# Thresholded attention and a two-layer network: where the weights are turned in the first rounds, and how the kernel starts and ends

## The chip, the cores and the metric

The kernel runs on one core of one Trainium2 chip. The core has five engines that each work through their own list of instructions in order: TensorE (PE in the profile; its weight loads are listed apart as PEld), VectorE (DVE), ScalarE (ACT), GpSimd (POOL) and SyncE (SP). They wait for each other only through semaphores. Matrix products land in PSUM, which has eight banks; DMA transfers are issued from a queue of an engine (here SP, ACT and POOL) and run beside the engines. The metric is the device time of one execution, in microseconds (us); lower is better.

## The reference

Eight batches of eight heads, 576 tokens each, 64 numbers to a head. Attention keeps only the scores that lie within `tau` of the row's maximum; its output goes through a network with a leaky ReLU between two layers.

```python
def _attn_ref(q, k, v, tau):                  # (8, 8, 576, 64) each, tau 0.02
    scores = np.matmul(q, k.transpose(0, 1, 3, 2)) / np.sqrt(64)
    thresh = np.max(scores, axis=-1, keepdims=True) - tau
    scores = np.where(scores >= thresh, scores, -1000000000.0)
    scores = scores - np.max(scores, axis=-1, keepdims=True)
    attn = np.exp(scores)
    attn = attn / (np.sum(attn, axis=-1, keepdims=True) + 1e-09)
    return np.matmul(attn, v).astype(np.float32)

def _moe_ref(x, w_in, w_out):                 # (4608, 512), (512, 2048), (2048, 512)
    h = x @ w_in
    g = np.maximum(0.01 * h, h)
    return (g @ w_out).astype(np.float32)
```

Between the two, the heads of a token are laid side by side, so that x has 4608 rows of 512.

## The kernel before

**Steps and rounds.** Heads are taken in pairs (four pairs a batch). The first 512 tokens of a batch are its main part, the last 64 its tail. A step is 128 queries of one pair against all 576 keys; `c` says which half of a block of 256 queries it is, so two steps with c = 0 and c = 1 share one set of weights, a `Pair` object. A batch has 18 steps (16 main, 2 tail), the whole 144. One loop, `while n < N + 7 ...` at the end of the kernel, with counter n, writes the program: a pass through it is called a round here. The order in which a round calls its functions is the order of each engine's list; nothing is moved later (`manual_schedule`).

**Inputs.** q and k come as 32-bit numbers and are used as a sum of two 16-bit halves, high and low (`split_now` with ACT and DVE for the first three pieces; `split_scale`, `split_high`, `split_low` on POOL for others). `turn` then transposes a piece on PE, 8 or 16 small transposes into a PSUM tile `tp` (tag "h", two banks, or "o", one), and copies it to `qT` or `kT` (lines 195, 189, 193), by ACT or by the engine that is given as `copy`. `units` gives the order of pieces: pair 0's k and q, the tail's k, pair 1's k and q, and so on; `first` is that list for batch 0, so that `first[7]` is the fourth pair's k. `load_pair` (line 477) issues a pair's load for batch 0; the first two go out on SP's queue (k) and on ACT's (q).

**A step.** In round n `scores` (L252) makes the step's scores in two PSUM tiles of two banks each, which are all that there are of that kind; so the next scores need DVE's `copy_min` (L260) to have emptied them. That copy also finds the row's extreme. `threshold` (L269 on DVE, L272 on POOL from step 28 on) adds tau. In round n + 1 `exps` makes the exponentials on ACT, for one head directly (L295) and for the other behind a sharp Prelu that drops what is under the threshold (L291, L292); `weights` (L304, DVE) does the dropping for the first head. Both leave their sums in `pr.sum`.

**Dividing and turning.** `recip` (L310, DVE) takes the reciprocals of the sums; `widen` (L313, DVE or POOL) writes them 64 times each into block 9 of the pair's weights `pr.w`, which blocks 0 to 8 fill with the weights of both heads (two times 576). Turned together with the weights, the reciprocals stand where the output needs them. From step 8 on the turning is one DMA transpose for a pair (`turn_w`, L321). The first eight steps are `early`: their weights are turned by PE (`turn_w_pe`, L331) into PSUM tiles `wp` of five blocks ("half" 0 is blocks 0 to 4 in bank "o", half 1 is blocks 5 to 9 in a bank "h") and copied to `wT` (L333). For an early step, `recip` and `widen` come in round n + 1 right behind `weights`, for one c at a time, and `turn_w_pe` in round n + 2. For later pairs they come in the round after, between `copy_min` and `threshold`, through the list `ended`. `pv` (L348) multiplies by v, `evacuate` (L370, L360) scales by block 9 into x; for early pairs this is in round 4, 6, 8 and 10.

**The network and the rest of a round.** `layer1` (L391, L393) and `layer2` (L407, L413) take finished groups of 256 or 128 tokens in small portions, one and two a round, from round 11 on; after the last step only these are left. `store` (L422, L425) sends a finished group out; the very last group is the tail rows of the last two batches, two stores of 64 rows. `idle` (L515) puts filler products on PE, in rounds 0 to 4 and in the even ones to 10 right behind the scores, in rounds 5, 7 and 9 behind the turning; `pool_at`, `turns_at`, `loads_at` and `rows_at` say in which round pieces of the preparation are put.

Of the kernel before, what the change touches and what calls it, by code (L numbers as in the profile page):

```python
# [37 lines left out]
def kernel(  # L38
# [236 lines left out]
    def exps(st):  # L275

        c = st.c
        if c == 0:
            pairs["now"] = pr = Pair()
            pr.w = sb.tile([128, 2, 10, 128], FP16, tag="w", bufs=3, name="w")  # L280
            pr.sum = sb.tile([128, 2, 2], FP32, tag="sum", bufs=3, name="sum")
            pr.n = 2
        st.pair = pr = pairs["now"]
        flat = pr.w[:, c, :, :].rearrange("q n d -> q (n d)")
        st.w = [flat[:, ds(576 * h, 576)] for h in range(2)]
        st.sum = [pr.sum[:, c, h : h + 1] for h in range(2)]
        st.e = sb.tile([128, 576], FP16, tag="e", bufs=2, name="e")
        for h in range(2):
            if h:
                z = st.s[:, h, :]  # L290
                nc.scalar.activation(out=z, in_=z, func=AF.Prelu, bias=st.th[:, h, 0:1], scale=-1.0, alpha=1e20)  # L291
                nc.scalar.activation(out=st.w[h], in_=z, func=AF.Exp, bias=minus_tau[:, :], scale=1.0,  # L292
                                     accum_out=st.sum[h])
            else:
                nc.scalar.activation(out=st.e[:, :], in_=st.s[:, h, :], func=AF.Exp, bias=st.mn[:, h, 0:1],  # L295
                                     scale=-1.0)
# [26 lines left out]

    def turn_w_pe(pr, c):
        if c == 0:
            new_wt(pr)
        for half, copy in enumerate((nc.scalar.copy, nc.scalar.copy if c else nc.vector.tensor_copy)):
            wp = ps.tile([128, 8, 128], FP16, tag="oh"[half], bufs=1 + half, name="wp")
# [69 lines left out]
    def layer2(n):  # L398
# [10 lines left out]
        if r == 7:  # L409
            nm = g.tokens // 128  # L410
            if m == 0:
                g.osb = sb.tile([128, nm, 512], FP32, tag=f"osb{nm}", bufs=2 if nm == 2 else 1, name="osb")
            nc.scalar.activation(out=g.osb[:, m, :], in_=g.o[:, :], func=AF.Copy, bias=0.0, scale=1.0)  # L413
            if m == nm - 1:
                stores.append(g)

    def store():
        g = stores.pop(0)
# [4 lines left out]
        else:  # L423
            for u in range(2):
                nc.sync.dma_start(out=out[ds((b + u) * S + MAIN, 64), :], in_=g.osb[ds(64 * u, 64), 0, :])  # L425

# [4 lines left out]
    def at(d, n, f):  # L431
        d.setdefault(n, []).append(f)
# [46 lines left out]

    load_pair(0, "k", nc.sync)  # L480
    load_pair(0, "q", nc.scalar)
    load_tails(0, "k", (nc.sync, nc.scalar))
# [36 lines left out]
    idle(34)  # L519
    for key in first[:3]:  # L520
        split_now(key)
    turn(first[0])
    turn(first[1], nc.vector.tensor_copy)
    turn(first[2], bank="o")
    idle(5)
# [10 lines left out]
    for n_, key in zip((1, 2, 3, 10), first[5:8] + first[9:]):  # L536
        at(turns_at, n_, lambda key=key: turn(key, nc.vector.tensor_copy if key[2] == "q" else None))

# [5 lines left out]
    while n < N + 7 or l1q or l2q or stores:  # L544
# [24 lines left out]
        if 0 < n < N:  # L569
            threshold(steps[n])  # L570
        if ended:
            widen(ended[0], 0, 2)
            turn_w(ended.pop())
# [4 lines left out]
        if 1 <= n <= N:  # L578
            last = steps[n - 1]
            weights(last)  # L580
            if last.early:
                recip(last.pair, last.c, 1)
                widen(last.pair, last.c, 1, nc.vector if n < 7 else nc.gpsimd)
            elif last.c == 1 and n < 2 * PERB:

# [7 lines left out]
        while stores:  # L593
            store()
        if l1q and l1q[0][3] <= n:
# [47 lines left out]
```

## Time and profile before

Three runs took 492.56, 492.96 and 493.05 us; the median is 492.96.

| | us |
|---|---|
| profiled execution | 492.28 |
| its span, first to last instruction | 490.3 |
| PE busy in the span | 475.4 |
| ACT busy | 432.7 |
| DVE busy | 406.9 |
| POOL busy | 315.2 |

Busy time by stretch of the span (us):

| stretch | PE | DVE | ACT | POOL |
|---|---|---|---|---|
| 0 to 8.7 (loads, first pieces) | 7.17 | 2.88 | 5.19 | 3.30 |
| 8.7 to 24.6 (rounds 0 to 4) | 14.44 | 15.00 | 13.77 | 15.15 |
| 24.6 to 44.2 (rounds 5 to 10) | 16.48 | 18.73 | 19.41 | 16.24 |
| 44.2 to 60 | 13.95 | 15.58 | 15.50 | 11.26 |
| 60 to 80 | 19.61 | 18.67 | 18.70 | 19.19 |
| 130 to 455 | 324.93 | 288.56 | 302.05 | 210.72 |
| 478.6 to 490.3 (last products, stores) | 7.18 | 0.00 | 1.85 | 0.00 |

How to read it: a row of the profile names the engine, the line of the kernel, the instruction, output<-input and the count; in brackets stands the idle time ahead of it and what ended that. Busy shares are means over stages with different limits, so each stage is read by itself. In the chain of waits every piece is what the next one waited for. PE's filler products count as busy, and matmuls are pipelined, so that a busy PE is not one at its peak. In the first rounds PE's busy time holds the filler.

### The profile page before, as it was taken

The page shows a single profiled execution, that of the slowest core. Times are in us where ns is not written, and L with a number is a line of the kernel's source. Part 1 is how long each engine was busy: PE and PEld are TensorE (multiplying, and loading weights), DVE is VectorE, ACT ScalarE, POOL GpSimd, SP SyncE. Part 2 cuts the span into 40 slices and gives each one's busy share as a digit, 9 for nine tenths or more (in the row PEclk, how much of TensorE's full clock was granted, in tenths as well). Part 3 has the DMA queues.
Part 4 walks back from the last instruction along what each step waited for, and adds up shares of the span by engine and source line. Part 5 has one row for each costly group of instructions (what it writes and reads, how often), then busy time and mean ns, then how long its engine had stood idle before and what let it go on. Part 6 is the DMA issues. An engine that isn't in the chain of part 4 may idle for free.

```text
span 490.3 us, 19692 instructions
## 1 busy us (share of the span) xinstructions
PE 475.4 (97%) x8039; PEld 343.6 (70%) x8039; DVE 406.9 (83%) x1217; ACT 432.7 (88%) x784; POOL 315.2 (64%) x534
## 2 busy tenths in 40 slices
PE   8989899999999999999999999999999999999996
PEld 6656666766777777777777777777777777667884
DVE  5999998989989899989899898989899898888100
ACT  6899999899999999999999999999999999999431
POOL 5987799678866686768766686768766673222000
PEclk9999999999999999999999999999999999999999
DMA  8999898989999998999997998999999978768412
GB/s 253 263 206 158 164 204 134 246 168 198 214 190 181 194 233 171 192 190 213 150 221 171 208 199 193 192 172 228 157 211 163 208 128 168 136 116 152 108 45 66
DMA packets 220443, 87.79 MB, mean 179 GB/s; under 512 B 190656, under 2 KB 217280, under 8 KB 220352
## 3 DMA queue, kind: packets, MB, share of 16 engines
q1 hardware_dynamic: 217120, 82.00, 81.8%
q0 software_dynamic: 2688, 4.19, 4.9%
q8 instruction: 63, 1.03, 0.9%
q10 hardware_dynamic: 544, 0.33, 0.2%
q14 instruction: 28, 0.23, 0.2%
HBM read 36.70 MB, written 9.44 MB: 94 GB/s over the span
## 4 chain that ended last, share of the span: by engine, by line
PE 78%; DVE 9%; ACT 4%; POOL 4%; DMA 2%; issue 2%; SPq 0%; POOLq 0%; DVEq 0%; ACTq 0%
PE hp L391 25%; PE o L407 20%; PE sc L252 20%; PE pv L348 7%; DVE s L260 5%; PE osc L407 4%; PE tpr L207 3%; DVE w L304 2%; POOL half L151 1%; DMA wT<-w 1%; DMA raw<-in_q_dram 1%; ACT w L292 1%; ACT e L295 1%; ACT s L291 1%; DVE x L370 1%
## 5 line engine op out<-in xcount | busy, mean ns | idle before, releaser
L260 DVE TENSOR_SCALAR_CACHE_REDUCE s<-sc 128x576 f32<-128x576 f32 x288 | 206.4, 753 | 33.4 <-PE sc L252 31.4
L252 PE MATMUL sc<-kT,qT 64*128 64x288 f16 (+1 forms) x1920 | 135.9, 285 | 4.2 <-DVE s L260 3.1
L391 PE MATMUL hp<-x,win 128*64 128x256 f16 x2048 | 136.7, 275 | 0.5 <-DVE x L370 0.5
L391 PEld LDWEIGHTS <-win 128*64 128x64 f16 x2560 | 118.5, 109 | 23.5 <-issue 17.4
L407 PE MATMUL o<-wout,g 128*64 128x512 f16 x992 | 127.8, 379 | 0.0
L304 DVE SCALAR_TENSOR_TENSOR w<-s,th,e 128x576 f16<-128x576 f32 x144 | 120.3, 835 | 0.5 <-ACT e L295 0.5
L272 POOL TENSOR_SCALAR th<-mn 128x2 f32<-128x2 f32 x116 | 52.7, 454 | 103.0 <-DVE s L260 81.2
L252 PEld LDWEIGHTS <-qT 64*128 64x128 f16 (+1 forms) x1920 | 77.0, 96 | 58.8 <-issue 43.6
L292 ACT ACTIVATE w<-s,minus_tau 128x576 f16<-128x576 f32 x144 | 111.7, 775 | 5.2
L291 ACT ACTIVATE s<-s,th 128x576 f32<-128x576 f32 x144 | 110.3, 766 | 1.9 <-POOL th L272 1.5
L295 ACT ACTIVATE e<-s,mn 128x576 f16<-128x576 f32 x144 | 110.2, 765 | 0.8 <-DVE s L260 0.8
L393 ACT ACTIVATE g<-hp 128x512 f16<-128x512 f32 x144 | 83.9, 583 | 26.2 <-PE hp L391 26.0
L151 POOL TENSOR_TENSOR half<-scaled,half 128x512 f16<-128x512 f32 (+1 forms) x91 | 89.3, 987 | 2.3
L407 PEld LDWEIGHTS <-g 128*64 128x64 f16 x1152 | 65.2, 110 | 29.8 <-issue 0.2
L348 PE MATMUL pv<-wT,v 128*64 128x256 f16 (+1 forms) x960 | 52.0, 247 | 0.5 <-DMA wT<-w 0.5
L348 PEld LDWEIGHTS <-v 128*64 128x64 f16 x960 | 41.6, 111 | 13.8 <-DMA wT<-w 1.2
L143 POOL CAST half<-scaled 128x512 f16<-128x512 f32 (+1 forms) x74 | 44.6, 602 | 4.5
L137 POOL TENSOR_SCALAR scaled<-raw 128x512 f32<-128x512 f32 x62 | 43.6, 702 | 5.4 <-DMA raw<-in_k_dram 4.4
L313 POOL CAST w<-rec 128x256 f16<-128x256 f32 (+1 forms) x70 | 32.0, 457 | 13.3 <-DVE rec L310 7.5
L106 POOL CAST v<-vraw 128x256 f16<-128x256 f32 x64 | 32.2, 532 | 1.3
L370 DVE TENSOR_TENSOR x<-pv,wT 128x256 f16<-128x256 f32 x64 | 27.1, 423 | 4.1 <-PE pv L348 4.0
L292 ACT ACTIVATION_READ_ACCUMULATOR w<-s,minus_tau 128x1 f32 x144 | 26.9, 187 | 0.0
(55 smaller groups left out, 323.1 us busy)
## 6 DMA issues: line engine op xcount, KB each, us to landing
vraw<-in_v_dram SPq DMA_DIRECT2D x16, 512.0 KB, 5.6
out_dram<-osb SPq DMA_DIRECT2D x16, 512.0 KB, 3.4
raw<-in_k_dram SPq DMA_DIRECT2D x14, 512.0 KB, 4.8
raw<-in_q_dram SPq DMA_DIRECT2D x14, 512.0 KB, 4.9
win<-in_moe_w_in_dram POOLq DMA_DIRECT2D x4, 512.0 KB, 7.3
wout<-in_moe_w_out_dram POOLq DMA_DIRECT2D x4, 512.0 KB, 13.8
wT<-w SPq DMA_TRANSPOSE x68, 5.9
raw<-in_k_dram SPq DMA_DIRECT2D x4, 256.0 KB, 5.0
```

The costliest lines, as they stand in the source:

```text
L151: nc.gpsimd.tensor_tensor(out=halves[key][:, 1, i : i + m, :, :], in0=src[:, i : i + m, :, :], in1=halves[key][:, 0, i : i + m, :, :], op= ...
L252: nc.tensor.matmul(out=o, lhsT=lhs, rhs=turned[st.b, "k"][rows, kx, pair, ds(key0, 288)], start=(i == 0), stop=(i == 2), skip_group_check= ...
L260: nc.vector.tensor_scalar(out=st.s[:, h, :].rearrange("p (a b) -> p a b", a=2), in0=st.sc[h][:, :, 0:288], scalar1=-1.0 / UNIT, scalar2=No ...
L272: nc.gpsimd.tensor_scalar(out=st.th[:, :, 0], in0=st.mn[:, :, 0], scalar1=1.0, scalar2=tau_f, op0=AX.mult, op1=AX.add)
L291: nc.scalar.activation(out=z, in_=z, func=AF.Prelu, bias=st.th[:, h, 0:1], scale=-1.0, alpha=1e20)
L292: nc.scalar.activation(out=st.w[h], in_=z, func=AF.Exp, bias=minus_tau[:, :], scale=1.0, accum_out=st.sum[h])
L295: nc.scalar.activation(out=st.e[:, :], in_=st.s[:, h, :], func=AF.Exp, bias=st.mn[:, h, 0:1], scale=-1.0)
L304: nc.vector.scalar_tensor_tensor(out=st.w[0], in0=st.s[:, 0, :], scalar=st.th[:, 0, 0:1], in1=st.e[:, :], op0=AX.is_le, op1=AX.mult, accum ...
L348: nc.tensor.matmul(out=o, lhsT=v16[st.b % 2][:, 2 * c + u if st.tail else st.p, blk, :], rhs=rhs, start=(i == 0), stop=(i == 4), skip_grou ...
L391: nc.tensor.matmul(out=hp[ds(64 * u2, 64), jj, :], lhsT=w_in16[:, i, ds(128 * j + 64 * u2, 64)], rhs=g.x[:, i, :], start=(i == 0), stop=(i ...
L393: nc.scalar.activation(out=g.g[:, ds(nj * u, nj), :], in_=hp[:, :, :], func=AF.Prelu, bias=0.0, scale=1.0, alpha=0.01)
L407: nc.tensor.matmul(out=g.o[ds(64 * u2, 64), :], lhsT=g.g[:, j, ds(128 * m + 64 * u2, 64)], rhs=w_out16[:, j, :], start=(j == 0), stop=(j = ...
```

## The change

Five places of the program are altered; what is computed stays the same.

1. The loads of the first pair's k and q are each cut in two by heads; the first head goes out on SP's queue, the second on ACT's, k ahead of q. The splitting of the tail's k moves behind the copy of the first turned piece, and of the first three turned pieces k and the tail's k are copied by DVE and q by ACT (before: k and the tail's k by ACT, q by DVE).
2. For the early pairs, reciprocal and widening are done once for both steps of a pair, through `ended`: the reciprocal right behind `copy_min` of the next odd round (3, 5, 7, 9), the widening behind that round's `threshold`, on DVE in rounds 3 and 5 and on POOL in rounds 7 and 9. Before, each early step had its own in the round behind it.
3. `turn_w_pe` turns only half 0 of c = 0 in the even round and the other three halves in the odd one (before: two and two). The engines of the four copies stay as they were, three on ACT and one on DVE.
4. The fourth pair's k, turned in round 3, is copied by DVE and not by ACT.
5. The last group's output bank is emptied by ACT (columns 0 to 255) and DVE (256 to 511), and the second of its two stores goes out on ACT's queue.

```diff
--- before.py
+++ after.py
@@ -280,6 +280,7 @@
             pr.w = sb.tile([128, 2, 10, 128], FP16, tag="w", bufs=3, name="w")
             pr.sum = sb.tile([128, 2, 2], FP32, tag="sum", bufs=3, name="sum")
             pr.n = 2
+            pr.early = st.early
         st.pair = pr = pairs["now"]
         flat = pr.w[:, c, :, :].rearrange("q n d -> q (n d)")
         st.w = [flat[:, ds(576 * h, 576)] for h in range(2)]
@@ -321,10 +322,14 @@
         nc.sync.dma_start_transpose(out=pr.wt[:, 0 : pr.n, :, :].rearrange("k c n q -> k (c n) q"),
                                     in_=pr.w[:, 0 : pr.n, :, :].rearrange("q c n d -> q (c n d)"))
 
-    def turn_w_pe(pr, c):
-        if c == 0:
+    def turn_w_pe(pr, step):
+
+        if step == 0:
             new_wt(pr)
-        for half, copy in enumerate((nc.scalar.copy, nc.scalar.copy if c else nc.vector.tensor_copy)):
+            parts = [(0, 0, nc.scalar.copy)]
+        else:
+            parts = [(0, 1, nc.vector.tensor_copy), (1, 0, nc.scalar.copy), (1, 1, nc.scalar.copy)]
+        for c, half, copy in parts:
             wp = ps.tile([128, 8, 128], FP16, tag="oh"[half], bufs=1 + half, name="wp")
             for i in range(5):
                 for u in range(2):
@@ -410,11 +415,14 @@
             nm = g.tokens // 128
             if m == 0:
                 g.osb = sb.tile([128, nm, 512], FP32, tag=f"osb{nm}", bufs=2 if nm == 2 else 1, name="osb")
-            nc.scalar.activation(out=g.osb[:, m, :], in_=g.o[:, :], func=AF.Copy, bias=0.0, scale=1.0)
+            half = 256 if n > N and g.tokens == 128 else 512
+            nc.scalar.activation(out=g.osb[:, m, 0:half], in_=g.o[:, 0:half], func=AF.Copy, bias=0.0, scale=1.0)
+            if half < 512:
+                nc.vector.tensor_copy(out=g.osb[:, m, half:512], in_=g.o[:, half:512])
             if m == nm - 1:
                 stores.append(g)
 
-    def store():
+    def store(n):
         g = stores.pop(0)
         b, t0 = g.where
         if g.tokens == 256:
@@ -422,7 +430,8 @@
             nc.sync.dma_start(out=rows[:, ds(t0, 2), :], in_=g.osb[:, :, :])
         else:
             for u in range(2):
-                nc.sync.dma_start(out=out[ds((b + u) * S + MAIN, 64), :], in_=g.osb[ds(64 * u, 64), 0, :])
+                eng = nc.scalar if u and n > N else nc.sync
+                eng.dma_start(out=out[ds((b + u) * S + MAIN, 64), :], in_=g.osb[ds(64 * u, 64), 0, :])
 
 
 
@@ -477,8 +486,11 @@
         eng.dma_start(out=raws[0, p // 2, which][:, ds(2 * (p % 2), 2), :],
                       in_=SRC[which][0, ds(2 * p, 2), 0:MAIN, :].rearrange("h (p t) d -> p h (t d)", t=4))
 
-    load_pair(0, "k", nc.sync)
-    load_pair(0, "q", nc.scalar)
+    for which in "kq":
+        raws[0, 0, which] = sb.tile([128, 4, 256], FP32, tag="raw", bufs=4, name="raw")
+        for h, eng in enumerate((nc.sync, nc.scalar)):
+            eng.dma_start(out=raws[0, 0, which][:, h, :],
+                          in_=SRC[which][0, h, 0:MAIN, :].rearrange("(p t) d -> p (t d)", t=4))
     load_tails(0, "k", (nc.sync, nc.scalar))
     load_pair(1, "k", nc.sync)
     load_pair(1, "q", nc.sync)
@@ -517,11 +529,12 @@
 
     first = units(0)
     idle(34)
-    for key in first[:3]:
-        split_now(key)
-    turn(first[0])
-    turn(first[1], nc.vector.tensor_copy)
-    turn(first[2], bank="o")
+    split_now(first[0])
+    split_now(first[1])
+    turn(first[0], nc.vector.tensor_copy)
+    split_now(first[2])
+    turn(first[1])
+    turn(first[2], nc.vector.tensor_copy, bank="o")
     idle(5)
     split_pool(first[3])
     for key in first[4:6]:
@@ -534,7 +547,7 @@
         at(pool_at, i if i < 2 else 1 + i // 2 if i < 6 else i, lambda i=i: load_w(i))
     at(turns_at, 0, lambda: turn(first[3], nc.vector.tensor_copy))
     for n_, key in zip((1, 2, 3, 10), first[5:8] + first[9:]):
-        at(turns_at, n_, lambda key=key: turn(key, nc.vector.tensor_copy if key[2] == "q" else None))
+        at(turns_at, n_, lambda n_=n_, key=key: turn(key, nc.vector.tensor_copy if n_ > 1 else None))
 
     N = len(steps)
 
@@ -568,7 +581,9 @@
             f()
         if 0 < n < N:
             threshold(steps[n])
-        if ended:
+        if ended and ended[0].early:
+            widen(ended.pop(), 0, 2, nc.vector if n < 7 else nc.gpsimd)
+        elif ended:
             widen(ended[0], 0, 2)
             turn_w(ended.pop())
         if n in rows_at:
@@ -578,10 +593,7 @@
         if 1 <= n <= N:
             last = steps[n - 1]
             weights(last)
-            if last.early:
-                recip(last.pair, last.c, 1)
-                widen(last.pair, last.c, 1, nc.vector if n < 7 else nc.gpsimd)
-            elif last.c == 1 and n < 2 * PERB:
+            if last.c == 1 and n < 2 * PERB:
 
                 ended.append(last.pair)
             elif last.c == 1:
@@ -591,7 +603,7 @@
         if n in rows_at:
             turned_now(0)
         while stores:
-            store()
+            store(n)
         if l1q and l1q[0][3] <= n:
             layer1()
         for f in turns_at.get(n, []):
```

## The prediction

> A round is one pass of the program's main loop (counter n), a step one tile of 128 queries of two heads; round n makes the scores of step n. A round's start is the start of its first score copy on DVE (L260).
>
> **What bounds the kernel now.** First the page's busy shares and granted clock.
> ```profile
> PE 475.4 (97%) x8039; PEld 343.6 (70%) x8039; DVE 406.9 (83%) x1217; ACT 432.7 (88%) x784; POOL 315.2 (64%) x534
> PEclk9999999999999999999999999999999999999999
> ```
> The shares hide the stages, so next the chain of waits, in order of time, for the first 60 us, where nearly all of the change lies:
> ```profile
> 28.65 0.17 DVE rec L310
> 28.83 0.02 issue
> 28.85 0.49 DVE w L313
> 29.34 1.36 DVE s L260 x4
> ...
> 30.73 0.16 DVE th L269 x2
> 30.90 0.75 DVE w L304 x2
> ```
> From 24.6 to 62.7 us the chain is DVE almost without a break (before that POOL's splits to 13.8, then ACT): score copy, threshold, weights and, each round, a reciprocal and a widening. So the change takes work off the engine that sets the early pace. Third the timeline, for what PE does meanwhile, in round 7:
> ```profile
> 31.69 0.78 PE L331 MATMUL wp<-ident,w 128*64 128x128 f16 x20
> 31.94 0.23 DVE L313 CAST w<-rec 128x128 f16<-128x128 f32 x1
> ...
> 32.81 0.75 DVE L260 TENSOR_SCALAR_CACHE_REDUCE s<-sc 128x576 f32<-128x576 f32 x1
> ...
> 34.30 0.89 PE L252 MATMUL sc<-kT,qT 64*128 64x288 f16 x11 [0.40 <-DVE s L260]
> ...
> 35.37 0.73 DVE L260 TENSOR_SCALAR_CACHE_REDUCE s<-sc 128x576 f32<-128x576 f32 x1
> ```
> PE turns the weights of step 5 (L331) at 31.69, before the score copy of round 7 begins at 32.81; it then waits for that copy (0.40) and makes the next scores while DVE does threshold and weights. PE's order is the program's, so what stands ahead of the next scores delays them.
> Starts of rounds 2 to 11, from the same view: 15.18, 19.22, 22.03, 25.70, 29.27, 32.81, 35.37, 38.66, 41.18, 44.15. Fourth, POOL's timeline, for the price of a widening there and for what carries a delay on:
> ```profile
> 45.83 0.93 POOL L313 CAST w<-rec 128x256 f16<-128x256 f32 x1 [2.01 <-DVE th L269]
> ...
> 55.57 0.61 POOL L191 COPY kT<-kT 128x512 f16<-128x512 f16 x1 [1.43 <-DVE kT L189]
> ...
> 64.75 0.39 POOL L313 CAST w<-rec 128x256 f16<-128x256 f32 x1
> ```
> POOL last waits for DVE at 55.57 (1.43); from there it runs without a gap to 79.25, and the chain goes over it, a DMA transpose of 6.04 and PE to the end. Last the two ends of the span:
> ```profile
> 2.04 0.84 SPq L477 DMA_DIRECT2D raw<-in_k_dram  x1
> 7.20 0.62 POOL L137 TENSOR_SCALAR scaled<-raw 128x512 f32<-128x512 f32 x1 [4.45 <-DMA raw<-in_k_dram]
> 9.62 0.64 PE L186 MATMUL tp<-ident,half 128*64 128x128 f16 x16
> 10.19 0.91 PE L252 MATMUL sc<-kT,qT 64*128 64x288 f16 x12
> ```
> POOL waits 4.45 for pair 1's k, splits it until 9.88; PE turns it and only then starts the scores of step 1.
> ```profile
> 485.81 0.60 ACT L413 ACTIVATE osb<-osc 128x512 f32<-128x512 f32 x1 [2.86 <-PE osc L407]
> 486.44 1.14 SPq L425 DMA_DIRECT2D out_dram<-osb  x2
> ```
> At the end ACT empties the last bank, then SP issues two stores one after the other, 0.57 each.
>
> **The change, part by part.**
>
> *First loads and order of the first splits.* One more DMA issue on each queue. The first pair's k may land up to 0.56 earlier in use: ACT starts on it at 4.34 now, and its own issues and table load (0.74 to 3.27, plus one issue of 0.51) end at 3.78. The exchanged copies (kT by DVE 0.69 for ACT 1.01, qT the other way, the tail's by DVE 0.42 for ACT 0.59) and the first lot of scores gain perhaps 0.3. I book nothing: step 1's scores wait for POOL at 9.88, and this cover hides it (uncovered it would be -0.3). What counts is what the extra issue is moved ahead of on SP: tail, pair 1's k and all behind, 0.51 later (0.47 and a gap). Bounds for POOL's start at 7.20: 0 (the load took 5.0 from issue, behind a backlog) to +0.5; I take +0.25.
>
> *Round 2.* Gone from DVE between 17.76 and 19.22: reciprocal, widening and the turned copy (0.47), which moves to round 3; left is qT's 0.60 to 0.68. Round 3 then starts at 18.35. PE has 10 transposes (0.29) less ahead of its scores and is ready. Gain 0.87, less 0.25: **-0.62** (bounds -0.9 to -0.4). The same removal in round 1 (0.7) gains only 0.1: scores of step 2 wait for POOL's 13.81.
>
> *Even rounds 4, 6, 8.* No reciprocal, no widening, half the transposes. Score copies, threshold, weights and output scaling took 2.62 where the trace has just these (58.65 to 61.27): 2.65 each. PE needs 0.55 filler + 0.29 + 0.65 pv + 1.11 scores = 2.60 after the round's start and fits.
>
> *Odd rounds 3, 5, 7, 9, where it turns.* The widening of a pair now stands behind the round's score copies, and PE's 30 transposes of the same round stand ahead of the next scores. The first 8 need no widening; the block holding the reciprocal does, and behind it on PE wait 20 more, the filler and the next scores, for which DVE waits. Price, round 7 or 9: score copies 1.35 (44.15 to 45.50), reciprocal to POOL's start 0.33 (45.50 to 45.83), POOL's widening of both halves 0.39 to 0.96, 0.07 to PE (40.08 to 40.15), 22 transposes 0.64 (20 took 0.58, 35.68 to 36.26), filler 0.55 (35.13 to 35.68), 12 scores 1.11 (11 took 1.03, 40.15 to 41.18, and 0.08). With 0.85 for the widening: **4.90** (4.44 to 5.2). I take 0.85, near the long row, because 0.93 was measured beside a weights instruction (45.70 to 46.51), and this one comes beside one too.
> The Trainium skill, "GPSIMD Engine Reference", 1. Specifications, says that GpSimd's SBUF interfaces are shared with VectorE and contended with its two-input instructions; were POOL held for all of the 0.74, a widening would be 1.13 and the sum 0.56 more over two rounds. The rows (0.39 and 0.93) agree with contention, not with its full price.
> Round 5: 1.35 + 0.12 + qT copy 0.60 + 0.08 + widening on DVE 0.45 (rows 0.23 and 0.52 for half of it) + 0.07 + 0.64 + 0.55 + 1.11 = **4.97** (4.75 to 5.3). Round 3: here the fourth pair's kT copy, moved to DVE, joins in. It takes 1.0 off ACT, which is then no longer last, but the last 10 transposes need its PSUM bank, and it waits behind the weights: 1.35 + 0.20 + 0.45 + 0.74 + 0.60 + 0.07 + 0.29 + 1.11 = **4.81** (4.6 to 5.1). Round 10 is unchanged, 2.97.
> Rounds 3 to 10: 4.81 + 2.65 + 4.97 + 2.65 + 4.90 + 2.65 + 4.90 + 2.97 = 30.50; now 44.15 - 19.22 = 24.93. **+5.57** (bounds +4.2 to +6.8).
>
> *What carries it.* From round 11 nothing is changed; DVE, POOL (whose waits for DVE move along) and PE follow later by the same.
>
> *The end.* Half the columns on each of two engines: ACT's 128x256 took 0.40 against 0.60, -0.2; DVE is idle there. The stores go out side by side: -0.57 of issue, some given back where 256 KB move together. **-0.7** (-0.9 to -0.5).
>
> Sum: -0.62 + 5.57 - 0.7 = **+4.25**. The profiled execution took 492.28 (span 490.3 and 1.98 around it): 496.5. It lies 0.68 under the median of 492.96, from which the sum gives 497.2; I forecast **496.9**. Bounds: +2.4 and +5.9, so 494.9 to 498.9 for this case alone.
>
> **Rivals.**
>
> *A, faster.* PE's wait is hidden and DVE's own work sets the pace: odd rounds then cost 1.35 + 0.12 + 0.60 + 0.08 + 0.45 + 0.74 + 0.40 = 3.74 (3 and 5) and 1.35 + 0.20 + 0.74 + 0.40 = 2.69 (7 and 9). Sum 23.78 against 24.93, -1.15; with -0.62 and -0.7 that is -2.5: 490.2. For it: DVE is the chain for 38 us and loses instructions. Against: it decides only if what PE does after the widening fits into DVE's 0.74 + 0.40, and the rows make it 0.64 + 0.55 + 1.11 = 2.30.
>
> *B, swallowed.* POOL's waits on DVE at 45.83, 51.92 and 55.57 (2.01 + 1.02 + 1.43 = 4.46) are slack in front of its unbroken run; if POOL ran ahead in them, 4.95 - 4.46 - 0.7 leaves -0.2: 492.8. For it: the run at 55.57 does set the later chain. Against: these waits are for DVE's results, which are late too.
>
> *C, the clock.* In odd rounds PE would stand for about 2.4 with only transposes around the gap; if it came back slow, as at the start (34 filler matmuls in 3.81, 112 ns each, against 69 in round 8), the 2.30 behind each wait become 3.7: four times 1.4, 502.5. Against: the granted clock is 1.00 throughout, and PE has no gap like this to judge by.
> The Trainium skill, "TensorE: Matmul & The Clock Gate", Why this matters for your kernels, warns of idle gaps over some 3 us, and its Part 4 that transposes do not count as busy; by that the gap is just at the edge. No run here shows it.
>
> **How the numbers follow.** Forecast 0.68, A 0.12, B 0.07, C 0.08, other mishaps 0.05. A measurement here tells from no change what is over about 0.2%, 1.0 us. Faster: A and a little, 0.13; same: B, 0.06; slower 0.81. The range must leave A, C and most of B out (0.2 and more), so it keeps the forecast's own 494.9 to 498.9 whole and 1.3 to 1.5 beside it for mis-sized waits: 493.6 to 500.4.
>
> **What would show it.** Right: round starts far apart in odd rounds (4.4 to 5.2) and near in even (2.6 to 2.7); round 3 at about 18.6 and round 11 at about 49; PE idle on the widening in L331, four times; DVE idle on scores in rounds 4, 6, 8, 10; POOL's two widenings near 0.9. The last store issued some 0.8 earlier against the last matmul. Wrong: round 11 at or before 44, or PE at L331 not waiting (A); round 11 late, but the run from 55.57 starting as now (B); scores in even rounds at 1.5 or more (C).

## The result, and the profile after

| | before | after |
|---|---|---|
| median (us) | 492.92 | 498.56 |
| lowest to highest, 6 runs each | 492.33 to 493.06 | 497.6 to 499.82 |
| profiled execution, its span | 492.28, 490.3 | 499.82, 497.8 |

The ratio is 1.0119, 95% interval 1.01 to 1.0137: the change costs about 5.6 us. The spread is wider as well: 2.2 us after against 0.7 before in these six executions each (of 15 executions of the kernel before beside experiment 1, one took 494.85).

The page of the changed kernel, busy time and granted clock:
```profile
PE 477.9 (96%) x8039; PEld 345.1 (69%) x8039; DVE 406.8 (82%) x1212; ACT 432.3 (87%) x782; POOL 315.3 (63%) x534
PEclk9997999999999999999999999999999999999999
```
DVE's work is as before and it has 5 instructions less; PE and its weight loads are busy longer, and the clock row, all nines before, has a 7 in the fourth slice (37.3 to 49.8 us). The loss lies where the change is. Starts of rounds 2 to 11 (first score copy of each, on DVE; the row before is from the prediction):

| round | 2 | 3 | 4 | 5 | 6 | 7 | 8 | 9 | 10 | 11 |
|---|---|---|---|---|---|---|---|---|---|---|
| before | 15.18 | 19.22 | 22.03 | 25.70 | 29.27 | 32.81 | 35.37 | 38.66 | 41.18 | 44.15 |
| after | 15.14 | 18.30 | 23.31 | 25.95 | 30.82 | 33.55 | 38.39 | 41.79 | 48.06 | 51.02 |

The changed kernel is ahead at round 3 and 6.87 behind at round 11. How an odd round loses, from its timeline of round 7 (start, length, engine, line, instruction; in brackets the idle time ahead of it and what ended it):
```profile
33.55 0.74 DVE L260 TENSOR_SCALAR_CACHE_REDUCE s<-sc 128x576 f32<-128x576 f32 x1
...
35.09 1.05 DVE L305 SCALAR_TENSOR_TENSOR w<-s,th,e 128x576 f16<-128x576 f32 x1
35.13 0.40 POOL L314 CAST w<-rec 128x256 f16<-128x256 f32 x1 [2.46 <-DVE rec L311]
35.58 0.81 PE L336 MATMUL wp<-ident,w 128*64 128x128 f16 x22 [2.03 <-POOL w L314]
36.32 0.62 PE L527 MATMUL idle<-ident 128*128 128x128 f16 x8
36.87 1.41 PE L252 MATMUL sc<-kT,qT 64*128 64x288 f16 x12
...
38.39 0.76 DVE L260 TENSOR_SCALAR_CACHE_REDUCE s<-sc 128x576 f32<-128x576 f32 x1 [1.84 <-PE sc L252]
```
PE stands 2.03 for the widening, which can't begin before the round's two score copies are over. Then it does 22 transposes, does its filler, and only then makes the scores that DVE waits 1.84 for. Before, DVE's next score copy came 2.56 after round 7's; now 4.84. The scores after the gap take 1.41 for 12, where 11 took 0.89 in the same round before. Round 9 has the same gap, with DVE and POOL the other way round:
```profile
43.34 0.81 DVE L305 SCALAR_TENSOR_TENSOR w<-s,th,e 128x576 f16<-128x576 f32 x1
43.48 0.94 POOL L314 CAST w<-rec 128x256 f16<-128x256 f32 x1 [4.46 <-DVE th L269]
44.47 1.38 PE L336 MATMUL wp<-ident,w 128*64 128x128 f16 x22 [2.45 <-POOL w L314]
```
The busy time by stretch (length, busy time of PE, PEld, DVE, ACT and POOL with counts, granted clock, DMA share, GB/s) shows the clock around these two:
```profile
34.00:36.90 2.90, 1.32 (x32) 1.13 (x34) 2.55 (x10) 2.14 (x5) 1.74 (x3) 1.00 1.17 238
36.90:40.20 3.30, 3.30 (x37) 2.34 (x38) 1.78 (x7) 2.97 (x6) 1.97 (x4) 0.53 1.24 208
40.20:44.40 4.20, 1.82 (x28) 1.05 (x24) 3.37 (x12) 2.66 (x5) 0.92 (x2) 0.91 1.24 205
44.40:47.50 3.10, 3.03 (x38) 2.44 (x40) 0.49 (x1) 2.13 (x4) 2.89 (x6) 0.52 0.15 24
47.50:51.00 3.50, 3.39 (x52) 2.24 (x49) 2.91 (x10) 3.27 (x6) 0.00 (x0) 1.00 0.02 5
```
It falls to about half twice. Taken in windows of 0.1 us, it is 0.50 from 37.1 to 40.5 and again from 44.0 to 47.4, and 1.00 on both sides of each. So each low stretch lasts 3.4 us, and its edges are not those of a gap: the first begins 1.5 after PE's wait of round 7 has ended (35.58), the second 0.5 before the wait of round 9 ends (44.47).

What carries the delay on: POOL's last wait for DVE, from POOL's timeline:
```profile
62.45 0.62 POOL L191 COPY kT<-kT 128x512 f16<-128x512 f16 x1 [1.43 <-DVE kT L189]
```
It reaches that copy 6.88 later than before (55.57) with the same wait of 1.43: all of the 6.87 is carried on. And the end of the changed kernel's timeline:
```profile
492.94 0.39 ACT L419 ACTIVATE osb<-osc 128x256 f32<-128x256 f32 x1 [2.85 <-PE osc L412]
493.36 0.42 DVE L421 COPY osb<-osc 128x256 f32<-128x256 f32 x1 [23.48 <-ACT osb L419]
493.81 0.50 SPq L434 DMA_DIRECT2D out_dram<-osb  x1
493.82 0.54 ACTq L434 DMA_DIRECT2D out_dram<-osb  x1
```
DVE does not begin beside ACT but when ACT is done. From the last bank's copy to the end of the span it was 490.3 - 485.81 = 4.49; it is 497.8 - 492.94 = 4.86.

### The profile page after: what moved, and what is told of

Read it like the earlier page. It is cut to its first block, busy times and chain, and to the rows that moved or that the text cites. A ratio compares the mean times of both kernels' runs of the same rounds, so it can differ in the third digit from the quotient of the medians.

```text
span 497.8 us, 19693 instructions
## 1 busy us (share of the span) xinstructions
PE 477.9 (96%) x8039; PEld 345.1 (69%) x8039; DVE 406.8 (82%) x1212; ACT 432.3 (87%) x782; POOL 315.3 (63%) x534
## 3 DMA queue, kind: packets, MB, share of 16 engines
q8 instruction: 63, 1.03, 0.8%
## 4 chain that ended last, share of the span: by engine, by line
PE 77%; DVE 8%; POOL 4%; ACT 4%; issue 3%; DMA 2%; SPq 0%; POOLq 0%; DVEq 0%; ACTq 0%
PE hp L396 25%; PE sc L252 20%; PE o L412 19%; PE pv L353 7%; DVE s L260 5%; PE osc L412 3%; PE tpr L207 3%; DVE w L305 2%; ACT s L292 1%; DMA wT<-w 1%; ACT e L296 1%; POOL half L151 1%; DMA rawt<-in_k_dram 1%; POOL v L106 1%; ACT w L293 1%
## 5 line engine op out<-in xcount | busy, mean ns | idle before, releaser
L314 POOL CAST w<-rec 128x256 f16<-128x256 f32 x70 | 32.9, 470 | 20.5 <-DVE th L269 10.8
```

## The experiments

Parts 1 to 5 are those of the list of the change. Ratios are against the kernel before, run on the same chip, with their 95% interval; times are medians.

**1. Everything but the widening.** The changed kernel with parts 2 and 3 undone.

```diff
-    def turn_w_pe(pr, step):
+    def turn_w_pe(pr, c):
...
-        if ended and ended[0].early:
-            widen(ended.pop(), 0, 2, nc.vector if n < 7 else nc.gpsimd)
-        elif ended:
+        if ended:
...
+            if last.early:
+                recip(last.pair, last.c, 1)
+                widen(last.pair, last.c, 1, nc.vector if n < 7 else nc.gpsimd)
```

> The changed kernel with parts 2 and 3 alone undone: each early step has its own reciprocal and widening again, right behind its weights, and two halves are turned a round. Theory W (PE's in-order wait for the widening in the odd rounds makes the loss): no wait on the widening is left, the lower granted clock goes with it, and the time comes back to about 493 us (492.5 to 494), since of the changed kernel's other parts only the end still costs (its last matmul to the end of the span took 4.86 us against 4.49). Rival (the loss lies in the first loads, the fourth pair's copy on VectorE or the end): it stays at 496 us or more.

493.36 (12 runs), ratio 1.0002 (0.9992 to 1.0012). All of the loss lies in parts 2 and 3, and the other three gain nothing that can be told. In its profiled execution, 495.59, the tail's k landed late (ACT waited 1.67 for it) and round 0 began at 10.71, against 8.71; that is one execution, the highest of the twelve. The expectation that the lower clock goes with the widening missed there: PE, with only transposes to do, waited 1.13 and 0.52 for that piece, and the granted clock was 0.50 from 8.1 to 11.5. Such a stretch does not need the late widening.

**2. The widening alone.** The kernel before with parts 2 and 3.

```diff
...
+            parts = [(0, 1, nc.vector.tensor_copy), (1, 0, nc.scalar.copy), (1, 1, nc.scalar.copy)]
...
+        if ended and ended[0].early:
+            widen(ended.pop(), 0, 2, nc.vector if n < 7 else nc.gpsimd)
...
-            if last.early:
-                recip(last.pair, last.c, 1)
-                widen(last.pair, last.c, 1, nc.vector if n < 7 else nc.gpsimd)
-            elif last.c == 1 and n < 2 * PERB:
+            if last.c == 1 and n < 2 * PERB:
```

> The kernel before with parts 2 and 3 alone: one reciprocal and widening a pair behind the odd round's score copies, three halves turned in that round. Theory W: nearly the whole loss, 496.5 to 499.5 us, with odd rounds 5, 7, 9 of 4.4 us or more, PE standing about 2 us before the turning, and a granted clock under 1.00 in some executions. Rival (the other parts): under 495 us.

497.92 (5 runs), ratio 1.0116 (1.0097 to 1.0135): the whole loss again. PE waits for the widening in round 5 (2.12), round 7 and round 9:
```profile
28.06 0.81 PE L336 MATMUL wp<-ident,w 128*64 128x128 f16 x22 [2.12 <-DVE w L314]
...
35.46 0.80 PE L336 MATMUL wp<-ident,w 128*64 128x128 f16 x22 [2.36 <-POOL w L314]
...
43.08 0.81 PE L336 MATMUL wp<-ident,w 128*64 128x128 f16 x22 [2.58 <-POOL w L314]
```
Rounds 5, 7 and 9 took 5.28, 4.34 and 5.69, of which round 7 lies just under the 4.4 that was expected. Only the last of the three waits brought a low clock (0.50 from 44.4 to 47.8); behind the first two it stayed at 1.00.

**3. Once per pair, but earlier.** The changed kernel, with reciprocal and widening of both steps right behind the weights of c = 1, at the end of the even round: nothing that PE turns in the odd round needs a widening of that round.

```diff
...
-            if last.c == 1 and n < 2 * PERB:
+            if last.early:
+                if last.c == 1:
+                    recip(last.pair, 0, 2)
+                    widen(last.pair, 0, 2, nc.vector if n < 7 else nc.gpsimd)
+            elif last.c == 1 and n < 2 * PERB:
```

> The changed kernel with the pair's one reciprocal and one widening moved ahead, behind the weights of its second step in the even round; three halves are still turned in the odd round. Theory W (the place of the widening behind the score copies is what costs): rounds 5, 7 and 9 fall to 2.7 to 3.4 us, no wait on the widening, 493.5 us (492 to 494.5); round 3 keeps a wait of about 1 us on the fourth pair's copy, for its PSUM bank. Rival (three halves in one round are too much for PE or its banks by themselves): the odd rounds stay over 4 us and the time over 496 us.

495.53 (5 runs), ratio 1.0055 (1.0042 to 1.0067). PE's wait for the widening shrinks to 0.30, 0.67 and 0.52 in rounds 5, 7 and 9, and half of the loss goes with it. But no such wait and 493.5 were expected, and both missed: rounds 7 and 9 came down to 2.69 and 3.09, round 5 only to 4.06, and round 3 took 4.74. In rounds 3 and 5 PE waits for something else ahead of the last 10 transposes:
```profile
22.11 0.47 PE L336 MATMUL wp<-ident,w 128*64 128x128 f16 x10 [1.69 <-DVE kT L195]
...
29.30 0.47 PE L336 MATMUL wp<-ident,w 128*64 128x128 f16 x10 [1.76 <-DVE qT L195]
```
These are waits for a turned input's copy, which still holds the PSUM bank ("h") that the third of the three halves needs. A piece of the preparation and two halves, three tiles, want the two banks of tag "h" in one round; before the change it was a piece and one half.

**4. The clock.** The changed kernel, in rounds 5, 7 and 9 with the filler (24 long and not 8) right behind the scores, so that it fills PE's gap, and none behind the turning.

```diff
-        if n < 11 and (n < 5 or n % 2 == 0):
-            idle(8 if n else 16)
+        if n < 11:
+            idle(16 if n == 0 else 24 if n > 4 and n % 2 else 8)
...
-        if 5 <= n < 11 and n % 2:
-            idle(8)
```

> The changed kernel with PE's filler of rounds 5, 7 and 9 moved from behind the turning to right behind the scores, ahead of the wait, and 24 products long for 8. Theory W with the clock as its second part: the granted clock stays at 1.00 in every execution, the executions lie within 0.5 us of each other instead of 2.2, and rounds 5, 7 and 9 each lose the filler's 0.55 us from their path: 495.5 to 496.5 us. If the lower clock does not come from PE standing, it is seen here as well and the spread stays; if the filler is not on the path, the fastest execution stays at 497.6 us.

495.75 (5 runs, 495.37 to 497.2), ratio 1.0067 (1.0054 to 1.008). By stretch (columns as above):
```profile
22.00:26.00 4.00, 4.00 (x50) 2.85 (x49) 2.30 (x8) 3.41 (x6) 3.75 (x7) 0.57 0.99 237
26.00:46.00 20.00, 18.10 (x334) 14.00 (x330) 16.67 (x56) 17.02 (x31) 13.41 (x25) 1.00 1.06 195
```
Where the gap is filled, from 26 on, the clock stays at 1.00 and rounds 5, 7 and 9 take 4.39, 3.80 and 4.43 (4.87, 4.84 and 6.27 without). Round 3, whose wait of 1.03 the filler does not fill, has the fall in its place: 0.57 in this window. The same wait of 1.03 in the changed kernel's round 3 brought none. So "1.00 in every execution" missed, and so did a spread of 0.5 us: it is 1.8. The edit does two things, covers the gap and takes 0.55 of filler from behind the turning, and the time alone does not tell them apart; the windows show the first, and experiment 8 tries the second without that gap.

**5. The start alone.** The kernel before with part 1.

```diff
-    load_pair(0, "k", nc.sync)
-    load_pair(0, "q", nc.scalar)
+    for which in "kq":
+        raws[0, 0, which] = sb.tile([128, 4, 256], FP32, tag="raw", bufs=4, name="raw")
+        for h, eng in enumerate((nc.sync, nc.scalar)):
+            eng.dma_start(out=raws[0, 0, which][:, h, :],
+                          in_=SRC[which][0, h, 0:MAIN, :].rearrange("(p t) d -> p (t d)", t=4))
...
-    for key in first[:3]:
-        split_now(key)
-    turn(first[0])
-    turn(first[1], nc.vector.tensor_copy)
-    turn(first[2], bank="o")
+    split_now(first[0])
+    split_now(first[1])
+    turn(first[0], nc.vector.tensor_copy)
+    split_now(first[2])
+    turn(first[1])
+    turn(first[2], nc.vector.tensor_copy, bank="o")
```

> The kernel before with part 1 alone (loads by heads on two queues, first splits and copies in the new order). Theory S (the tail's k, now issued 0.4 us later and split behind the first copy, holds the first scores until about 9.1 us, but the scores of step 2 still wait for POOL, so nothing is left by round 2): round 0 starts 0.2 to 0.5 us later, round 2 within 0.15 us of 15.18, the time within 0.2% of before (492.3 to 493.5), with some executions 1 to 3 us longer where the tail's k lands late, PE stands and the granted clock falls. Rival (the earlier first k shortens the start): round 2 starts 0.3 us or more earlier and the time is 492.5 or less.

492.03 (11 runs), ratio 0.9995 (0.9985 to 1.0005): no difference. ACT's first split begins at 3.69 (4.34 before), but the tail's k then waits 1.08 for its load, and round 0 begins at 8.75 (8.71 before). What the first piece wins, the third gives back. By the words set down before the run it is the rival that came true, since round 2 begins at 14.83 (0.35 earlier) and the time is under 492.5. But that gain can't be told from chance: in the profiled executions without part 1 (the kernel before, experiments 2, 6 and 10) round 2 begins between 14.79 and 15.28, and in those with it between 14.83 and 15.15, or at 17.05 where the tail's k was late (experiment 1).

**6. The fourth pair's k alone.** The kernel before with part 4.

```diff
-        at(turns_at, n_, lambda key=key: turn(key, nc.vector.tensor_copy if key[2] == "q" else None))
+        at(turns_at, n_, lambda n_=n_, key=key: turn(key, nc.vector.tensor_copy if n_ > 1 else None))
```

> The kernel before with part 4 alone (the fourth pair's k copied by VectorE). ACT is the chain from 14.2 to 24.6 us in the kernel before and loses 1.0 us there, DVE takes 0.6 to 0.7. If ACT sets that stage: round 5 starts 0.3 to 0.9 us earlier and the time falls to 492.0 to 492.6. Rival (DVE is as late as ACT): round 5 at 25.7 or later, 492.7 to 493.5.

492.85 (11 runs), ratio 1.0008 (0.9999 to 1.0017): no difference that can be told, and no gain: the time lies in the rival's range. By itself part 4 costs nothing that can be told; under part 2 the copy stands behind the widening and the weights on DVE.

**7. The end with tiles of its own.** The kernel before; the last bank is emptied by ACT and DVE into two separate SBUF tiles, with four stores.

```diff
-            nc.scalar.activation(out=g.osb[:, m, :], in_=g.o[:, :], func=AF.Copy, bias=0.0, scale=1.0)
+            if n > N and g.tokens == 128:
+                g.osc = [sb.tile([128, 256], FP32, name=f"osc{i}") for i in range(2)]
+                nc.scalar.activation(out=g.osc[0][:, :], in_=g.o[:, 0:256], func=AF.Copy, bias=0.0, scale=1.0)
+                nc.vector.tensor_copy(out=g.osc[1][:, :], in_=g.o[:, 256:512])
...
+        elif n > N:
+            for u in range(2):
+                for i, eng in enumerate((nc.sync, nc.scalar)):
+                    eng.dma_start(out=out[ds((b + u) * S + MAIN, 64), ds(256 * i, 256)], in_=g.osc[i][ds(64 * u, 64), :])
...
```

> The kernel before with part 5 alone, but ACT and DVE write to output tiles of their own, and four stores of 64 rows by 256 columns go out, two on each queue. In the changed kernel DVE began its half 0.42 us after ACT had begun, when ACT had ended. Theory O (the wait comes from the output tile that both wrote): here DVE begins within 0.1 us of ACT, and the last matmul is followed by 4.5 us or less to the end of the span. Theory P (it comes from the PSUM tile that both read): DVE still begins only when ACT has ended, and the end takes 4.8 us or more. The time as a whole says nothing at this size: 492.3 to 493.5 in both.

493.0 (11 runs), ratio 1.0015 (1.0006 to 1.0024), slower by a little. The two copies, in the timeline of the end:
```profile
486.59 0.38 ACT L415 ACTIVATE osc<-osc 128x256 f32<-128x256 f32 x1 [2.86 <-PE osc L407]
487.01 0.42 DVE L416 COPY osc<-osc 128x256 f32<-128x256 f32 x1 [23.48 <-ACT osc L415]
```
They still go one after the other with nothing shared but the PSUM tile `osc` that they read (the names of input and output are alike here). From the copy to the end of the span it is 491.4 - 486.59 = 4.81, as theory P has it.

**8. Early, and the filler ahead.** Experiment 3 with the 8 filler products of rounds 5, 7 and 9 moved from behind the turning to behind the scores.

```diff
-        if n < 11 and (n < 5 or n % 2 == 0):
-            idle(8 if n else 16)
+        if n < 11:
+            idle(16 if n == 0 else 8 if n > 4 and n % 2 else 8)
...
-        if 5 <= n < 11 and n % 2:
-            idle(8)
```

> The changed kernel with the widening moved ahead into the even round, as in the run before, and with the 8 filler products of rounds 5, 7 and 9 right behind the scores. Theory B (what is left of the loss is the third half's wait for its PSUM bank in rounds 3 and 5): both waits of about 1.7 us stay, rounds 3 and 5 stay at 3.8 us or more, 494.3 to 495.5 us. Rival (the filler behind the turning was what is left): 493.5 us or less.

493.87 (5 runs), ratio 1.0036 (1.0023 to 1.005): between theory B (494.3 or more) and its rival (493.5 or less), so that neither was wholly right. Against experiment 3 the ratios differ by 0.0019, some 0.9 us, and their intervals overlap (by the medians 1.66, but the kernel before stood 0.57 lower beside this one). Of the two waits on a bank only one is as long as it was:
```profile
22.28 0.75 PE L336 MATMUL wp<-ident,w 128*64 128x128 f16 x10 [1.68 <-DVE kT L195]
22.96 1.62 PE L252 MATMUL sc<-kT,qT 64*128 64x288 f16 x12
...
30.61 0.47 PE L336 MATMUL wp<-ident,w 128*64 128x128 f16 x10 [0.67 <-DVE qT L195]
```
Round 5's went from 1.76 to 0.67; by which way the filler did that was not followed. The second row is worth a look: 12 scores took 1.62 behind a wait of 1.68, where experiment 3 took 0.91 behind one of 1.69; its profiled execution, 496.24, is 2.4 above the median. There the granted clock was 0.50 from 22.3 to 25.7.

**9. And a bank of its own.** Experiment 8 with the third half of the odd round in the bank of tag "pv".

```diff
-            wp = ps.tile([128, 8, 128], FP16, tag="oh"[half], bufs=1 + half, name="wp")
+            wp = ps.tile([128, 8, 128], FP16, tag="pv" if c * half else "oh"[half], bufs=1 if c * half else 1 + half, name="wp")
```

> The kernel of the run before with one word changed more: the third half of the odd round is turned into the bank of the pv tile and not into one of the two that the preparation's pieces use. Theory B: no wait for a copy is left on PE in rounds 3 and 5, rounds 3 and 5 at 3.0 to 3.6 us, 492.3 to 493.3 us, so 1.5 to 2.5 us less than that run. Rival: no difference of more than 0.5 us between the two.

492.56 (11 runs), ratio 1.0007 (0.9998 to 1.0016): 1.3 us less again (1.5 to 2.5 was expected), and level with the kernel before. Rounds 3 and 5 took 3.58 and 3.17. Round 3 on PE, timeline:
```profile
19.64 1.00 PE L336 MATMUL wp<-ident,w 128*64 128x128 f16 x30
20.58 0.91 PE L252 MATMUL sc<-kT,qT 64*128 64x288 f16 x12
```
All 30 transposes go through without a wait and the scores follow. In round 5 only the scores still wait 0.39, for the turned q that they read. Rounds 3 to 10 take 44.41 - 18.74 = 25.67; before, 24.93.

**10. The best of it on the kernel before.** The kernel before with the early widening, its filler and bank, and part 4, but without parts 1 and 5.

```diff
...
+            parts = [(0, 1, nc.vector.tensor_copy), (1, 0, nc.scalar.copy), (1, 1, nc.scalar.copy)]
...
+                if last.c == 1:
+                    recip(last.pair, 0, 2)
+                    widen(last.pair, 0, 2, nc.vector if n < 7 else nc.gpsimd)
...
```

> The kernel before with one reciprocal and one widening a pair, behind the weights of its second step in the even round, three halves turned in the odd round with the third one in the bank of the pv tile, the filler of rounds 5, 7 and 9 right behind the scores, and the fourth pair's k copied by VectorE. In the run before with the early widening, PE waited 1.69 us in round 3 and 1.76 us in round 5 for a copy that stood in the bank which the third half needs. Theory W with that bank as its second part: neither wait is left, rounds 3 and 5 fall under 3.5 us, and the time is 492.0 us (491 to 493.3). Rival (three halves in one round cost PE too much as such): rounds 3 and 5 stay over 4 us and the time at 494.5 us or more.

492.17 (11 runs), ratio 1.0002 (0.9993 to 1.0011). One reciprocal and one widening a pair are worth nothing here, even where nobody waits for them: rounds 3 to 10 take 44.23 - 18.55 = 25.68, 0.75 more than before, and round 3 starts 0.67 earlier (18.55 for 19.22).

**11. Start, and two queues at the end.** The kernel before with part 1; ACT empties the whole last bank, the second store goes out on ACT's queue.

```diff
-                nc.sync.dma_start(out=out[ds((b + u) * S + MAIN, 64), :], in_=g.osb[ds(64 * u, 64), 0, :])
+                eng = nc.scalar if u and n > N else nc.sync
+                eng.dma_start(out=out[ds((b + u) * S + MAIN, 64), :], in_=g.osb[ds(64 * u, 64), 0, :])
...
```

> The kernel before with part 1 and, of part 5, only the second store on ACT's queue; ACT empties the whole bank. Theory P (the shared PSUM tile made ACT and DVE take turns, 0.82 us for 0.60, and the rest of part 5 gains): the last matmul's end to the end of the span takes 4.0 to 4.3 us, against 4.5 before and 4.9 with both; the time 491.7 to 492.5 us, which rounds of this size do not tell from before. Rival (two stores side by side gain nothing, since the second one's data move together with the first's): 4.5 us again.

492.06 (11 runs), ratio 0.9996 (0.9988 to 1.0005). The issues do start together, as this kernel's timeline shows:
```profile
485.53 0.50 SPq L426 DMA_DIRECT2D out_dram<-osb  x1
485.53 0.54 ACTq L426 DMA_DIRECT2D out_dram<-osb  x1
```
Its DMA issues at the end (queue, count, KB, median us from issue to landing) show what becomes of it:
```profile
out_dram<-osb SPq DMA_DIRECT2D x1, 128.0 KB, 2.4
out_dram<-osb ACTq DMA_DIRECT2D x1, 128.0 KB, 2.7
```
Each store took 2.4 or 2.7; one after the other they took 2.3. From the copy to the end of the span it is 489.5 - 484.90 = 4.60 against 4.49 before: nothing gained, and the 4.0 to 4.3 of theory P missed. No version tried lies under the kernel before by more than the runs can tell.

## Why the prediction was right or wrong

**The sign and the main term were right.** In experiments 1 and 2 the loss goes and comes with the late widening; experiment 3, which leaves the rest and makes it earlier, takes half of it away. The mechanism is the one forecast: in rounds 5, 7 and 9 PE's 30 transposes, with the widening ahead of the last 22, stand in front of the next scores; in round 3 PE waits instead (1.03) for the copy of the fourth pair's k, whose bank the last 10 need, which was forecast too. Predicted and measured, in us:

| round | predicted | after |
|---|---|---|
| start of 3 | 18.6 | 18.30 |
| 3 | 4.81 | 5.01 |
| 4 | 2.65 | 2.64 |
| 5 | 4.97 | 4.87 |
| 6 | 2.65 | 2.73 |
| 7 | 4.90 | 4.84 |
| 8 | 2.65 | 3.40 |
| 9 | 4.90 | 6.27 |
| 10 | 2.97 | 2.96 |

Rounds 3 to 7 add up to 20.09 where 19.98 was predicted. For rounds 3 to 6 the terms bear that out, but in round 7 it is luck. The widening took 0.40 there where 0.85 was booked, and the scores behind it took 1.52 (36.87 to 38.39), mostly in the low clock, where round 5's took 1.02 (29.80 to 30.82). Experiment 2, with the same 0.40 and the full clock in round 7, took 4.34.

**Rival A fell**: PE waits for the widening, and DVE for the scores. **Rival B fell**: POOL's unbroken run started 6.88 later. **Rival C, at 0.08, came in part.** Rounds 8 and 9 hold 2.12 more than the terms allow, and in both the granted clock was halved. With the 0.50 hidden in round 7 (1.52 for 1.02), the first low stretch cost 1.25 (0.50 + 0.75). The second cost 1.28: in round 9 the 22 transposes, the filler and the scores took 3.59 from 44.47 to 48.06, where round 5's took 2.31 (28.51 to 30.82). So the price of 1.4 an event was near, but not every gap brought one: of four waits two did in the profiled execution. Over six executions of the changed kernel, median 498.56, the two whose whole-span clock is 1.00 took 497.69 and 497.6, 4.7 over the median before, near the +4.25 of the sum; those at 0.991 to 0.995 took 498.56 to 499.82, so 0.9 to 2.2 more. The spread thus goes with the clock; no version that keeps the late widening and holds the clock in every execution was made. The forecast was a case without the clock, with the events beside it; in four of six executions about one event or more belonged into it.

**The start** was mis-sized by a little: POOL's start was booked at +0.25 and came at 7.06, 0.14 earlier than before. That no gain was booked for the earlier first split (3.72, expected by 3.78) was right, for one more reason than was given: the tail's k came late and round 0 began 0.40 later than before, but POOL's split hid that, and round 2 began at 15.14.

**POOL's widening**, booked at 0.85 in both rounds, was 0.40 in round 7 and 0.94 in round 9. In round 7 POOL was spared and the weights on DVE, issued 0.04 ahead of it, took 1.05; in round 9, DVE 0.14 ahead, DVE took 0.81 and POOL was held. The Trainium skill, "SBUF — State Buffer", SBUF: two separate sides, says that the pair of ports which the two share is locked by one for a whole instruction, so that the other is held, not slowed. These rows agree with one paying for both; experiment 2's trace has the same 0.40 and 0.94, and no run tried it apart.

**The step that failed in sign is the end**: "Half the columns on each of two engines: ACT's 128x256 took 0.40 against 0.60, -0.2; DVE is idle there. The stores go out side by side: -0.57 of issue". In place of -0.7 the stretch came out 0.37 longer. That is no accident of one execution: in five profiled executions with the old end (the kernel before, experiments 2, 5, 6 and 10) it took 4.41 to 4.76, in six with the new one (the changed kernel, experiments 1, 3, 4, 8 and 9) 4.82 to 4.92. The two copies run one after the other, 0.39 + 0.42 for 0.60, with output tiles of their own too (experiment 7), so an idle DVE is no use there. And the stores' 0.57 of issue was saved at the queue but not at the landing (experiment 11): issued together, 128 KB take 2.4 and 2.7 from issue instead of 2.3, which puts the last landing 0.17 earlier than before (485.53 - 484.90 + 2.7 = 3.33 after the copy's start; before, 486.44 - 485.81 + 0.57 + 2.3 = 3.50), and the span then ends 1.27 after it, where it was 1.0. Why that last piece grew stays open: the profile has no row for it, and in experiment 5, with the old end, it was 1.27 too (490.5 - 486.36 - 0.57 - 2.3). The trace of before had told of the copies. This row of its timeline, with ACT reading the same tile, was overlooked (columns as in the timelines above):
```profile
7.67 0.42 DVE L193 COPY kT<-tp 128x512 f16<-128x512 f16 x1 [0.25 <-ACT kT L189]
```
DVE waits for ACT's copy from the same PSUM tile `tp`; both only read it, they write different columns of kT, and PE's last product into it had ended at 6.91.

The sum as worked out was thus +4.95 to round 11 and -0.7 at the end. Without the clock, the rows give +4.34 (4.95, 0.30 less at the start, 0.17 more in rounds 3 to 6, 0.56 less in round 7, 0.09 more in round 9, 0.01 less in round 10) and +0.37, or +4.7, as in the two executions with a clock of 1.00. The rest of the profiled execution's +7.54 is the 2.53 of the clock and 0.3 that no row was found for (7.13 at the last bank's copy against 6.88 at POOL's run, and 0.04 outside the span). So the sum came near partly because errors cancel: the start gained 0.30 more and round 7's widening cost 0.45 less than booked, against 1.07 more at the end. The forecast of 496.9 is 1.7 under the median, and 498.56 lies within its range. (The bound of 494.9 in it does not follow from its terms, since 492.28 + 2.4 is 494.7 and 492.96 + 2.4 is 495.4, but the measured time is far from it.)

Of the signs named beforehand, round 11 came at 51.02 for about 49, PE's long waits for the widening were three and not four, one of POOL's two widenings was near 0.9, and the last store was issued 0.32 earlier against the last bank's copy and not 0.8 (1.20 before, 0.88 after).

What remained of the loss once the widening was early is explained by two things: the PSUM bank of the third half (experiment 9 against 8, side by side: 1.3 us, intervals apart) and, less surely, 8 filler products behind the turning (experiment 8 against 3: about 0.9, intervals overlapping). The sum had the filler in rounds 5, 7 and 9 and the bank in round 3 only.

## What to carry to other kernels

Taking an instruction off the engine that sets the pace gains nothing when what replaces it stands ahead of the next round's input on another engine's in-order list: follow that list, position by position, before counting the saving. Moving a batch of small work into every second round needs the place (engine order, PSUM banks, filler) for a double portion there. And two engines split over the columns of one PSUM tile should be expected to take turns, unless a row of the trace shows them side by side.

## What the runs showed of the hardware

**The granted clock fell to 0.50 for 3.4 us at a time, about stretches in which PE had nothing but transposes and gaps.** Every low stretch of the traces shown here has that length: two in the changed kernel, whose starts lie 6.8 apart, and one each in experiments 1, 2, 4 and 8. The length of the wait alone does not decide. The clock fell about waits of 1.03 (experiment 4), 1.13 (1), 1.68 (8), 2.03, 2.45 and 2.58 (2), and it did not about 1.03 and 2.01 (the changed kernel), 1.69 and 1.76 (3), 2.12 and 2.36 (2). Counted with the transposes beside it, from the last other product to the next, the stretch was 3.2 to 4.4 us long where the clock fell and 3.5 to 4.1 in these six where it did not; the kernel before has none over 2.1 in the first 50 us, and its clock stayed at 1.00. What decides among the long ones was not found. The Trainium skill, "TensorE: Matmul & The Clock Gate", Part 1, has half rate after one idle window of about 3.4 us. The halved rate agrees with the traces; that it takes a gap of 3 us (its Why this matters for your kernels) agrees only if the transposes beside the gap are counted into it.

**Copying one PSUM tile with two engines took 0.39 + 0.42 for 0.60.** The Trainium skill, "PSUM — Partial Sum Buffer", PSUM bank collisions raise a hardware error, says that two engines must not touch one bank in the same partitions at a time, columns apart or not, and that the compiler orders them. The 0.39 and 0.42 in a row agree.

**A second DMA queue saved 0.57 at the issue and 0.17 at the landing**, and nothing at the end of the span.
